# GT in five pieces of 512 columns and a turned strip, in place of ten pieces of 320

## The chip, the cores and the metric

The kernel runs on one core of a Trainium2 chip. A core has TensorE (PE in the profile, with PEld for its weight loads), VectorE (DVE), ScalarE (ACT), GpSimd (POOL) and SyncE (SP), each with an instruction queue of its own that runs in order, and DMA queues that SyncE and GpSimd feed. Times are device microseconds (us). The metric is the median time of the runs, and a profile of one execution goes with it.

## The reference

The output mixes two blocks over the same input x of 2,048 tokens by 640 columns; everything is float32.

```python
def _A_ref(x, wqkv, wo):            # 32 heads of 20 columns
    qkv = (x @ wqkv).reshape(B, S, 3, H, Dh).transpose(2, 0, 3, 1, 4)
    q, k, v = qkv[0], qkv[1], qkv[2]
    phi = lambda t: jnp.where(t > 0, t + 1, jnp.exp(t)) + 1e-6
    pq, pk = phi(q), phi(k)
    kv = jnp.einsum("bhsd,bhse->bhde", pk, v)
    z = jnp.einsum("bhsd->bhd", pk)
    num = jnp.einsum("bhqd,bhde->bhqe", pq, kv)
    den = jnp.einsum("bhqd,bhd->bhq", pq, z)[..., None] + 1e-6
    return (num / den).transpose(0, 2, 1, 3).reshape(B, S, D) @ wo
def _B_ref(x, w_gate, w_up, w_down):    # 1,536 hidden columns
    h = _sigmoid(x @ w_gate) * (x @ w_up)
    return h @ w_down
x = A_x
g = _sigmoid((x * gate_w).sum(-1, keepdims=True))
return g * _A_ref(x, A_wqkv, A_wo) + (1 - g) * _B_ref(x, B_w_gate, B_w_up, B_w_down)
```

## The kernel before

**Arithmetic.** A product is made of three matmuls (`mm3`, L407 to L409 in the profile): each operand is split into a high and a low part, and high by high, low by high and high by low are summed. A split takes ScalarE a copy to the high part (L420) and VectorE a subtraction for the low part (L424). So `woh`, `wol` are the two parts of rows of `wo`, `pkh`, `pkl` those of phi(k), `xnh`, `xnl` those of x.

**Phase 1.** No v is computed for the tokens. Since kv = pk^T (x Wv) = (pk^T x) Wv, the kernel accumulates GT = x^T pk, a 640 by 640 matrix, over the 16 tiles of 128 tokens, and multiplies it by Wv afterwards. `gt` lies in SBUF as 128 partitions by 5 blocks by 640 columns: rows are the columns of x, columns are those of k. The class `GTBatch` makes it in five batches: the tiles of block 0, of blocks 1 and 2, 3 and 4, 5 and 6, and (`glast`) of block 7, a block being two tiles. In each batch there is a result in PSUM for every unit u, one of five row blocks and one of two halves of 320 columns: ten units. `part` issues a unit's matmuls for some tiles, `out` adds the result to `gt` (a copy in the first batch). Between the units `order.fill()` lets other work in.

**The q steps.** Phase 1 is followed by `q_phase(1)`, a row of steps j = 0, 1, 2, ... that compute q for half of the tokens; its matmuls read splits of x's forms (`xah`, `xbh`, `xrh`, `xth`, `b12h`, ...) and of the weights' forms (`wg`, `wu`, `ws`, which are staged in `wst` and sent on to DRAM). Lists `extra[j]` put other work ahead of step j. `kv_part(hg)`, for six groups of heads that are 120 or 100 columns wide, multiplies `wv_sb` with the group's columns of `gt` (matmul L1578), masks the result with `bd` (`kvt`) and splits it (`kvh`, `kvl`). `m_part(hg)`, at j = 5, 6, 8, 10, 12 and 13, multiplies that with the group's rows of `wo`: six matmuls of 320 columns, whose results ScalarE copies to `ms` and GpSimd stores to `m_dram`.

**What sets the order.** The program's text doesn't fix all of it. A planner, the class `Order`, keeps estimated times for TensorE, ScalarE and VectorE as the program is built. Work that is not bound to a place is queued with its costs, perhaps with a key and a time from which it is ready; `fill` emits a queued item when its estimated end lies within a set slack of TensorE's. Items queued with `first=True` are looked at before others. `need(key)` emits an item at once if it has not been emitted yet. `queue_wo(hg)` queues the split of a group's rows of `wo` in this way, with the key ("wo", hg); `m_part(hg)` begins with `need(("wo", hg))` and ends with `queue_wo(hg + 2)`. All engines then run what was emitted, in that order. PSUM has eight result slots, rot0, rot1, dd0, dd1, ch0, ch1, cc0 and cc1; two of a name are used in turn (`ps_tile`).

Of the kernel before, what the change touches and what calls it, by code (L numbers as in the profile page):

```python
# [14 lines left out]
P = 128  # L15
# [4 lines left out]
TG = 512  # L20
# [347 lines left out]
def a_cost(w):  # L368
    return 0.06 + w / 1200

def v_cost(w):
    return 0.07 + w / 960

@with_exitstack
def gated_mix_kernel(ctx: ExitStack, tc: tile.TileContext, xt, xn, wk, wv, wo, wst_q, wst_f, out_t):
# [90 lines left out]
    z_dram = dram.tile([P // H, H, DH], F32, name="z_dram")  # L466
    m_dram = dram.tile([D, D], F32, name="m_dram")
    mr_dram = dram.tile([P, KC, D], F32, name="mr_dram")
    bdn = HPG * DH
# [504 lines left out]
    def queue_split(b):  # L974
        for s in range(2):
            order.add(a_cost(D), v_cost(D), lambda s=s: k_split(tok(b, s)), ("pk", b))

    class GTBatch:
        def __init__(self, n, blocks):
# [3 lines left out]
        def part(self, u, t0, t1, tag="rot", out=True):  # L983
            m, h = divmod(u, 2)
            cs = slice(h * HALF, (h + 1) * HALF)
            ms = slice(m * P, (m + 1) * P)
            if u not in self.ps:
                self.ps[u] = ps_tile(tag)
            ps = self.ps[u][:, :HALF]
            for n in range(t0, t1):  # L990
                i = self.tiles[n]
                mm3(ps, XN[i][0][:, ms], XN[i][1][:, ms], PK[i][0][:, cs], PK[i][1][:, cs],
                    n == 0, n == len(self.tiles) - 1)
            if t1 == len(self.tiles) and out:
                self.out(u)

        def out(self, u):
            m, h = divmod(u, 2)
            ps, dst = self.ps[u][:, :HALF], gt[:, m, h * HALF:(h + 1) * HALF]
            if self.n == 0 and u < 4:  # L1000
# [80 lines left out]
    order.slack(True)  # L1081
    for u in range(2 * KC):
        g.part(u, 0, 2, "rot" if u % 2 else "dd")
        order.fill()
# [3 lines left out]
    for c in range(1, 4):  # L1088
# [79 lines left out]
        else:  # L1168
            queue_xn(7)
        for u in range(6 if c == 1 else 4):  # L1170
            g.part(u, 0, 2, ("rot", "dd", "ch", "cc")[u % 4])
            if c == 1 and u == 0:
# [15 lines left out]
        for u in range(2 * KC):  # L1188
            g.part(u, 2 if u in g.ps else 0, len(g.tiles),
                   ("rot", "dd", "rot", "cc")[u % 4] if c == 3 or u < 8 else "rot")  # L1190
            order.fill()
            if u in (3, 5, 7, 9,):
                order.run("qw")
            if c == 2 and u == 9:
# [1812 lines left out]
```

## Time and profile before

| | before |
|---|---|
| median of 3 runs | 724.65 us (724.34 to 724.76) |
| span of the profiled execution | 722.5 us |
| median less span | 2.1 us |
| ScalarE, VectorE, TensorE busy in the span | 51%, 81%, 99% |
| DMA | 261 GB/s over the span |

The execution that was profiled is known by its span, from the first instruction to the last; its own time is not given apart. The stretch of the last batch of GT ends at 140.99 us of the span, and the first group of `m_part` begins at 157.66. Three more rows of the profile's groups show what the evacuations and the copies of `gt` are like: the operation, its operands, how often, its busy time in us and the mean of one in ns, then the idle time of the engine ahead of it and who ended that.

```profile
L424 DVE TENSOR_TENSOR tb<-rot,tb 128x512 f32<-128x512 f32 x56 | 36.1, 682 | 0.3 <-PE rot L409 0.3
L420 ACT ACTIVATE c<-ch 128x512 f32<-128x512 f32 x54 | 32.3, 597 | 84.2 <-PE ch L409 83.4
L424 DVE TENSOR_TENSOR hf<-c,hf 128x512 fp32r<-128x512 f32 x80 | 54.4, 687 | 19.3 <-ACT hf L420 18.9
```

### The profile page before, as it was taken

The page shows a single profiled execution, that of the slowest core. Times are in us where ns is not written, and L with a number is a line of the kernel's source. Part 1 is how long each engine was busy: PE and PEld are TensorE (multiplying, and loading weights), DVE is VectorE, ACT ScalarE, POOL GpSimd, SP SyncE. Part 2 cuts the span into 40 slices and gives each one's busy share as a digit, 9 for nine tenths or more (in the row PEclk, how much of TensorE's full clock was granted, in tenths as well). Part 3 has the DMA queues.
Part 4 walks back from the last instruction along what each step waited for, and adds up shares of the span by engine and source line. Part 5 has one row for each costly group of instructions (what it writes and reads, how often), then busy time and mean ns, then how long its engine had stood idle before and what let it go on. Part 6 is the DMA issues. An engine that isn't in the chain of part 4 may idle for free.

```text
span 722.5 us, 10190 instructions
## 1 busy us (share of the span) xinstructions
PE 718.2 (99%) x3539; PEld 616.7 (85%) x3539; DVE 587.1 (81%) x1028; ACT 370.0 (51%) x686; POOL 114.0 (16%) x184
## 2 busy tenths in 40 slices
PE   9999999999999999999999999999999999999998
PEld 8999999988888888888888888888888888888886
DVE  6898888988677989898989977447696968799895
ACT  6884748367556654545364664354423242454451
POOL 0211112113311212111210224001010101002200
PEclk9999999999999999999999999999999999999999
DMA  7677689598787866757687899968989895959947
GB/s 258 162 230 182 179 196 286 129 357 280 273 303 259 325 241 234 262 221 264 244 321 273 255 313 360 404 222 292 364 256 309 247 395 182 407 217 332 217 101 240
DMA packets 81690, 191.31 MB, mean 265 GB/s; under 512 B 12154, under 2 KB 40202, under 8 KB 77926
## 3 DMA queue, kind: packets, MB, share of 16 engines
q1 hardware_dynamic: 60726, 117.72, 49.6%
q0 software_dynamic: 20624, 72.70, 30.2%
q8 instruction: 28, 0.46, 0.3%
q10 hardware_dynamic: 288, 0.23, 0.1%
q14 instruction: 24, 0.20, 0.1%
HBM read 113.14 MB, written 75.20 MB: 261 GB/s over the span
## 4 chain that ended last, share of the span: by engine, by line
PE 99%; DMA 0%; DVE 0%; ACT 0%; issue 0%
PE ch L407 11%; PE ch L409 11%; PE ch L408 11%; PE cc L409 9%; PE cc L407 9%; PE cc L408 9%; PE dd L407 7%; PE dd L408 7%; PE dd L409 7%; PE rot L407 5%; PE rot L408 5%; PE rot L409 5%; PE rot L1578 1%; PE dd L2735 1%; PE ch L2735 0%; DMA xnh<-wk 0%
## 5 line engine op out<-in xcount | busy, mean ns | idle before, releaser
L420 ACT ACTIVATE c<-ch 128x512 f32<-128x512 f32 x54 | 32.3, 597 | 84.2 <-PE ch L409 83.4
L424 DVE TENSOR_TENSOR hf<-c,hf 128x512 fp32r<-128x512 f32 x80 | 54.4, 687 | 19.3 <-ACT hf L420 18.9
L420 ACT ACTIVATE hf<-c 128x512 fp32r<-128x512 f32 x80 | 48.9, 624 | 31.1 <-DVE c L424 31.0
L424 DVE TENSOR_TENSOR c<-cc,c 128x512 f32<-128x512 f32 x42 | 28.9, 688 | 28.3 <-PE cc L409 17.4
L407 PE MATMUL ch<-xth,ws 128*128 128x512 f32 x112 | 43.6, 389 | 0.0
L408 PE MATMUL ch<-xtl,ws 128*128 128x512 f32 x112 | 43.6, 389 | 0.0
L409 PE MATMUL ch<-xth,ws 128*128 128x512 f32 x112 | 43.6, 389 | 0.0
L424 DVE TENSOR_TENSOR c<-c,c 128x512 f32<-128x512 f32 x52 | 35.7, 687 | 3.3 <-ACT c L420 2.7
L424 DVE TENSOR_TENSOR tb<-rot,tb 128x512 f32<-128x512 f32 x56 | 36.1, 682 | 0.3 <-PE rot L409 0.3
L407 PE MATMUL dd<-xrh,wg 128*128 128x512 f32 x90 | 35.2, 391 | 0.0
L408 PE MATMUL dd<-xrl,wg 128*128 128x512 f32 x90 | 35.1, 390 | 0.0
L409 PE MATMUL dd<-xrh,wg 128*128 128x512 f32 x90 | 35.0, 389 | 0.0
L420 ACT ACTIVATE c<-dd 128x512 f32<-128x512 f32 x22 | 13.1, 596 | 41.4 <-PE dd L409 41.4
L407 PE MATMUL cc<-xbh,ws 128*128 128x512 f32 x84 | 32.7, 389 | 0.0
L408 PE MATMUL cc<-xbl,ws 128*128 128x512 f32 x84 | 32.7, 389 | 0.0
L409 PE MATMUL cc<-xbh,ws 128*128 128x512 f32 x84 | 32.7, 389 | 0.0
L424 DVE TENSOR_TENSOR tb<-dd,tb 128x512 f32<-128x512 f32 x36 | 24.7, 686 | 9.3 <-PE dd L409 9.2
L420 ACT ACTIVATE dd<-ch 128x512 f32<-128x512 f32 x22 | 12.8, 582 | 35.9 <-PE ch L409 35.9
L424 DVE TENSOR_TENSOR tb<-cc,tb 128x512 f32<-128x512 f32 x36 | 24.5, 684 | 1.9 <-PE cc L409 1.9
L424 DVE TENSOR_TENSOR wst<-wst 128x256 f32<-128x256 f32 (+1 forms) x65 | 24.6, 396 | 1.4
L409 PEld LDWEIGHTS ch<-xth,ws 128*128 128x128 f32 x112 | 21.0, 188 | 4.7 <-DVE ws L424 0.3
L408 PEld LDWEIGHTS ch<-xtl,ws 128*128 128x128 f32 x112 | 21.0, 188 | 4.3
(703 smaller groups left out, 2378.9 us busy)
## 6 DMA issues: line engine op xcount, KB each, us to landing
wf<-ws POOLq DMA_DIRECT2D x12, 1152.0 KB, 7.5
ws<-wf SPq DMA_DIRECT2D x11, 1152.0 KB, 8.8
wst<-wst_f SPq DMA_DIRECT2D x12, 640.0 KB, 4.9
wf<-wg POOLq DMA_DIRECT2D x12, 640.0 KB, 6.1
wd<-wd POOLq DMA_DIRECT2D x12, 640.0 KB, 8.1
wg<-wf SPq DMA_DIRECT2D x12, 640.0 KB, 6.9
wf<-wd SPq DMA_DIRECT2D x10, 640.0 KB, 11.0
xnst<-xn SPq DMA_DIRECT2D x16, 320.0 KB, 4.5
```

The lines of the kernel that those rows point to most:

```text
L407: nc.tensor.matmul(out, l_hi, r_hi, start=first, stop=False, skip_group_check=True)
L408: nc.tensor.matmul(out, l_hi, r_lo, start=False, stop=False, skip_group_check=True)
L409: nc.tensor.matmul(out, l_lo, r_hi, start=False, stop=last, skip_group_check=True)
L420: nc.scalar.activation(out, src, fn, **kw)
L424: nc.vector.tensor_tensor(out, a, b, op=op)
L1578: nc.tensor.matmul(ps[:w, :w], v[:, m, :w], gt[:, m, c0:c0 + w], start=(m == 0), stop=(m == KC - 1))
L2735: nc.tensor.matmul(ps, l, r, start=new, stop=j == 1 and k == ks[-1], skip_group_check=True)
```

## The change

The first 512 columns of GT are made in five units, one for each row block, 512 columns wide. The last 128 columns are made the other way round: pk's 128 columns are now the rows of the result and x's 640 columns run along it, in two units of 384 and 256 columns (`STRIP`). What arrives in `gt[:, m, 512:]` is thus a transposed block. After the last batch's two strip units, `gt_turn` turns it back: VectorE transposes within squares of 32 by 32, GpSimd writes the result to a new DRAM tensor `gt_dram` and reads it back in four pieces with the squares in their places, and ScalarE copies that to `gt`. The copy has the key "turn"; `extra[7]` needs it ahead of step 7. The heads' groups 4 and 5, which read columns from 512 on, move from steps 6 and 8 to 8 and 9, and group 3 stays.

```diff
+    gt_dram = dram.tile([P, D], F32, name="gt_dram")
...
+    STRIP = {KC: (0, 3), KC + 1: (3, KC)}
+    NU = KC + 2
+
+    def gt_turn():
+
+        turned = m1_tile("mb", "turned")
+        order.on_vec(D, "", 1.0, turned, gt[:, :, TG:])
+        nc.vector.transpose(turned.rearrange("p (b m c) -> p m b c", m=KC, c=H),
+                            gt[:, :, TG:].rearrange("p m (b c) -> p m b c", c=H))
+        gp.dma_start(gt_dram, turned)
+        back = m1_tile("mb", "back")
+        src = gt_dram.rearrange("(a r) (b n) -> b r a n", r=H, b=P // H)
+        for b in range(P // H):
+            gp.dma_start(back[b * H:(b + 1) * H].rearrange("r (a n) -> r a n", a=P // H), src[b])
+        order.add(a_cost(D), 0, lambda: act(gt[:, :, TG:].rearrange("p m (a c) -> p a m c", c=H),
+                                            back.rearrange("p (a m c) -> p a m c", m=KC, c=H), AF.Copy),
+                  "turn", lambda: order.when(back) + 1, first=True)
...
         def part(self, u, t0, t1, tag="rot", out=True):
-            m, h = divmod(u, 2)
-            cs = slice(h * HALF, (h + 1) * HALF)
-            ms = slice(m * P, (m + 1) * P)
             if u not in self.ps:
                 self.ps[u] = ps_tile(tag)
-            ps = self.ps[u][:, :HALF]
             for n in range(t0, t1):
-                i = self.tiles[n]
-                mm3(ps, XN[i][0][:, ms], XN[i][1][:, ms], PK[i][0][:, cs], PK[i][1][:, cs],
-                    n == 0, n == len(self.tiles) - 1)
+                x, pk = XN[self.tiles[n]], PK[self.tiles[n]]
+                if u < KC:
+                    ms = slice(u * P, (u + 1) * P)
+                    ps, l, r = self.ps[u], [t[:, ms] for t in x], [t[:, :TG] for t in pk]
+                else:
+                    b0, b1 = STRIP[u]
+                    ps = self.ps[u][:, :(b1 - b0) * P]
+                    l, r = [t[:, TG:D] for t in pk], [t[:, b0 * P:b1 * P] for t in x]
+                mm3(ps, *l, *r, n == 0, n == len(self.tiles) - 1)
...
-    tags = ["rot", "rot", "ch", "ch", "dd", "dd", "cc", "cc", "rot", "rot"]
-
-    for u in range(4):
+    tags = ["ch", "dd", "dd", "cc", "cc", "rot", "ch"]
+
+    for u in (KC, KC + 1, 0):
         glast.part(u, 0, 2, tags[u])
-    for u in range(4, 10):
+    order.add(0, v_cost(D), gt_turn, "turned", first=True)
+    for u in range(1, KC):
         glast.part(u, 0, 2, tags[u], out=False)
         order.fill()
-        if u == 5:
+        if u == 1:
             wg_split(("q", 1, KC - 1), w_stage)
-        elif u == 8:
-            glast.out(4)
-            glast.out(5)
-    p1_tail = [lambda u=u: glast.out(u) for u in range(6, 10)]
+        elif u == 3:
+            glast.out(1)
+    p1_tail = [lambda u=u: glast.out(u) for u in range(2, KC)] + [lambda: order.need("turned")]
...
-    for hg, (j, t) in enumerate(((1, "rot"), (1, "rot"), (3, "cc"), (6, "rot"), (6, "rot"), (8, "rot"))):
+    for hg, (j, t) in enumerate(((1, "rot"), (1, "rot"), (3, "cc"), (6, "rot"), (8, "rot"), (9, "rot"))):
         extra[j].append(lambda hg=hg, t=t: kv_part(hg, t))
+    extra[7].append(lambda: order.need("turn"))
```

The units of the batches between are issued in the same way, with other PSUM slots. The planner reckons with all of this, and so the order changes beyond the lines of the diff. Three places of it follow, one on each of three engines. A row names the line, the operation, its result and operands (with numbers of their tiles) and the shape of the result.

**TensorE, two units of one batch.** Before, in the last batch, the two tiles of one unit of 320 columns:

```order
L407 MATMUL rot0_1725<-pkh_1628,xnh_1600 128x320
L408 MATMUL rot0_1725<-pkl_1629,xnh_1600 128x320
L409 MATMUL rot0_1725<-pkh_1628,xnl_1601 128x320
L407 MATMUL rot0_1725<-pkh_1632,xnh_1625 128x320
L408 MATMUL rot0_1725<-pkl_1633,xnh_1625 128x320
L409 MATMUL rot0_1725<-pkh_1632,xnl_1626 128x320
```

After, in the last batch, from the second tile of the strip's unit of 256 columns (`ch1_1582`) to the whole of the first unit of 512:

```order
L407 MATMUL ch1_1582<-xnh_1503,pkh_1511 128x256
L408 MATMUL ch1_1582<-xnl_1504,pkh_1511 128x256
L409 MATMUL ch1_1582<-xnh_1503,pkl_1512 128x256
L407 MATMUL ch0_1590<-pkh_1507,xnh_1500 128x512
L408 MATMUL ch0_1590<-pkl_1508,xnh_1500 128x512
L409 MATMUL ch0_1590<-pkh_1507,xnl_1501 128x512
L407 MATMUL ch0_1590<-pkh_1511,xnh_1503 128x512
L408 MATMUL ch0_1590<-pkl_1512,xnh_1503 128x512
L409 MATMUL ch0_1590<-pkh_1511,xnl_1504 128x512
```

Where ten such units of six matmuls stood in the last batch, there are now seven. In the strip the moving operand is x and the one that is loaded is pk; over the whole kernel TensorE has 144 matmuls fewer.

**VectorE, in the q steps, around wol of group 0.** Before (`wol_1934` is group 0's, `wol_1966` group 1's):

```order
L424 TENSOR_TENSOR kvl_1911<-kvt_1908,kvh_1910 120x120
L424 TENSOR_TENSOR wol_1934<-wo_sb_1837,woh_1933 120x640
L424 TENSOR_TENSOR wst_1826<-wst_1826 128x256 x2
L424 TENSOR_TENSOR wst_1826<-wst_1826 128x128
L424 TENSOR_TENSOR xst_89<-xst_89 128x512
L428 SCALAR_TENSOR_TENSOR qe_1932<-qe_1932,qr_1944 128x512
L424 TENSOR_TENSOR wol_1966<-wo_sb_1841,woh_1965 120x640
```

After (`wol_1838` is group 0's; group 1's, `wol_1874`, follows two ws later; `qe_1778` is what was `qe_1964` before, made from the result rot0 of the same step):

```order
L428 SCALAR_TENSOR_TENSOR qe_1778<-qe_1778,qr_1792 128x512
L424 TENSOR_TENSOR kvt_1802<-cc1_1796,bd_65 100x100
L856 CAST kvh_1804<-kvt_1802 100x100
L424 TENSOR_TENSOR kvl_1805<-kvt_1802,kvh_1804 100x100
L424 TENSOR_TENSOR wst_1654<-wst_1654 128x256 x2
L424 TENSOR_TENSOR wst_1654<-wst_1654 128x128
L424 TENSOR_TENSOR xst_90<-xst_90 128x512
L424 TENSOR_TENSOR xz_1421<-xz_1421 128x512
L424 TENSOR_TENSOR xtl_1414<-xst_90,xth_1413 128x2x256
L424 TENSOR_TENSOR c11_1818<-dd0_1811,c11_1818 128x512
L424 TENSOR_TENSOR wol_1838<-wo_sb_1665,woh_1837 120x640
```

Group 0's wol has moved from ahead of the qe of the step's first result to behind c11, which reads the result (dd0) of the matmuls directly ahead of group 0's `m_part`.

**ScalarE, the same stretch and the next.** Before, from the stretch's start (woh of groups 0 and 1):

```order
L420 ACTIVATE wu_1885<-wst_1826 128x384
L420 ACTIVATE woh_1933<-wo_sb_1837 120x640
L420 ACTIVATE qe_1932<-dd1_1916 128x512
L420 ACTIVATE qr_1944<-dd1_1916 128x512
L420 ACTIVATE woh_1965<-wo_sb_1841 120x640
```

After, first the strip's copy and what is behind it, then woh of groups 0 and 1, then that of group 2:

```order
L420 ACTIVATE gt_86<-back_1629 128x4x5x32
L420 ACTIVATE qe_1754<-dd1_1738 128x512
L420 ACTIVATE qr_1758<-dd1_1738 128x512
L420 ACTIVATE wg_1779<-wst_1654 128x640
L420 ACTIVATE wu_1781<-wst_1654 128x384
```

```order
L420 ACTIVATE c11_1818<-ch0_1810 128x512
L420 ACTIVATE xth_1413<-xst_90 128x2x256
L420 ACTIVATE woh_1837<-wo_sb_1665 120x640
L420 ACTIVATE xth_1413<-xz_1421 128x2x256
L420 ACTIVATE ws_1849<-wst_1654 128x640
L420 ACTIVATE ws_1849<-wst_1654 128x512
L420 ACTIVATE ms_1843<-cc0_1844 120x320
L420 ACTIVATE ms_1843<-cc1_1860 120x320
L420 ACTIVATE woh_1873<-wo_sb_1669 120x640
```

```order
L420 ACTIVATE ms_1883<-dd1_1884 120x320
L420 ACTIVATE ms_1883<-dd0_1891 120x320
L420 ACTIVATE c22_1919<-ch1_1678 128x512
L420 ACTIVATE woh_1928<-wo_sb_1841 100x640
L420 ACTIVATE ms_1934<-dd1_1935 100x320
```

The woh of groups 0 and 1 have moved behind the results of the step ahead of their products, and that of group 2 stands behind c22, which reads the result (ch1) of the matmuls directly ahead of group 2's products. The copy of the strip stands ahead of the qe of dd1.

More of the change, by code (lines that the diff above doesn't have):

```diff
@@ L1081, in gated_mix_kernel @@
     order.slack(True)
-    for u in range(2 * KC):
+    for u in range(NU):
         g.part(u, 0, 2, "rot" if u % 2 else "dd")
@@ L1169, in gated_mix_kernel @@
             queue_xn(7)
-        for u in range(6 if c == 1 else 4):
-            g.part(u, 0, 2, ("rot", "dd", "ch", "cc")[u % 4])
+        first = 4 if c == 1 else 3
+        for u in range(first):
+            g.part(u, 0, 2, ("rot", "dd", "ch", "cc")[u])
             if c == 1 and u == 0:
@@ L1187, in gated_mix_kernel @@
             queue_forms(nx)
-        for u in range(2 * KC):
-            g.part(u, 2 if u in g.ps else 0, len(g.tiles),
-                   ("rot", "dd", "rot", "cc")[u % 4] if c == 3 or u < 8 else "rot")
+        for u in range(NU):
+            g.part(u, 2 if u in g.ps else 0, len(g.tiles), ("rot", "dd", "ch", "cc", "dd", "rot", "rot")[u])
             order.fill()
-            if u in (3, 5, 7, 9,):
+            if u > 2:
                 order.run("qw")
-            if c == 2 and u == 9:
+            if c == 2 and u == NU - 1:
                 queue_ls()
```

10 lines of the change are left out of this document (7 added, 3 removed).

## The prediction, made before the changed kernel was run

> **What bounds the kernel now.** I read the page first (span, busy shares, granted clock, the chain that ended last), then TensorE's waits, then the timeline around the end of GT and the first steps of q.
>
> ```profile
> span 722.5 us, 10190 instructions
> PE 718.2 (99%) x3539; PEld 616.7 (85%) x3539; DVE 587.1 (81%) x1028; ACT 370.0 (51%) x686; POOL 114.0 (16%) x184
> PEclk9999999999999999999999999999999999999999
> PE 99%; DMA 0%; DVE 0%; ACT 0%; issue 0%
> PE rot L496 <- PEq L2998: 0.8, 1, 0.8
> PE ch L1022 <- DVE k1h L855: 0.2, 1, 0.2
> ```
>
> TensorE is busy for 99% of the span at full granted clock. The last two lines are its whole list of waits (total, times, longest, in us): 0.8 and 0.2, both at the start. So the time is the sum of the matmuls' steps. Two things can change it: what the matmuls take, and a wait that TensorE does not have today. A faster VectorE or ScalarE brings nothing; a later one can cost at once. The profiled execution is given by its span alone, 722.5; the median of the timed runs, 724.65 (724.34 to 724.76), is 2.1 above it, which I take for what lies around the span in every run. The terms below are changes of the span; I add them to 722.5 and then the 2.1, which is the same as adding them to 724.65.
>
> **Term 1: the matmuls of GT.** Their price is the distance of starts, not the duration shown, since matmuls overlap.
>
> ```profile
> 130.40 0.31 PE L407 MATMUL dd<-pkh,xnh 128*128 128x320 f32 x1
> 140.85 0.30 PE L409 MATMUL rot<-pkh,xnl 128*128 128x320 f32 x1
> ...
> 146.76 0.40 PE L408 MATMUL dd<-xrl,wg 128*128 128x512 f32 x1
> 149.71 0.39 PE L409 MATMUL dd<-xah,wg 128*128 128x512 f32 x1
> ...
> 715.44 0.28 PE L407 MATMUL rot<-pq,ws 128*128 128x256 f32 x1
> 718.91 0.28 PE L409 MATMUL rot<-hf,wf 128*128 128x256 f32 x1
> ```
>
> Between the first two rows lie 71 steps of 320 columns: 10.45/71 = 0.1472 us. Between the next two, 13 of 512: 0.2269. Between the last, 29 of 256: 0.1197. For 384 no row exists; the line between 320 and 512 gives 0.1472 + 64 × 0.000415 = 0.1738. Per token tile of 128, before has 30 × 0.1472 = 4.416; after has 15 × 0.2269 + 3 × 0.1738 + 3 × 0.1197 = 4.284. That is 0.13 us for each of 16 tiles: **2.1 us less**. The columns streamed stay 9,600 per tile; what goes is the fixed part of 9 matmuls, about 14 ns each. If 384 falls on the line from 256 to 512 instead (0.1733), the gain is the same to a tenth; I take 1.8 to 2.2.
>
> The Trainium skill ("TensorE: Matmul & The Clock Gate", section "Wait — 56ns, not 53.3ns?") puts the fixed part of a warm matmul at about 2.5 ns; 144 matmuls fewer would then bring an estimated 0.4 us and not 2.1. The rows above disagree, and the rows decide, as these are this kernel's own operands.
>
> **Evacuations.** Ten results per batch become seven, on VectorE and ScalarE, which are not the bound. I walked GT's batches and the key/value products of head groups 0 to 2 with the pitches above: each result slot is free 0.3 us or more ahead of its next matmul. Cost 0; at the tightest place a late add would cost a few tenths.
>
> **Term 2: three new waits for wo's splits.** In the order of after, woh (ScalarE) and wol (VectorE) of head groups 0, 1 and 2 are issued directly ahead of the products that read them; before, groups 0 and 1 have theirs microseconds earlier.
>
> ```profile
> 146.53 0.74 ACT L420 ACTIVATE woh<-wo_sb 120x640 fp32r<-120x640 f32 x1 [0.76 <-DMA wo_sb<-wo]
> 149.97 0.82 DVE L424 TENSOR_TENSOR wol<-wo_sb,woh 120x640 fp32r<-120x640 f32 x1
> ...
> 153.11 0.39 PE L409 MATMUL rot<-b12h,wg 128*128 128x512 f32 x1
> 157.43 0.39 PE L409 MATMUL dd<-xrh,wg 128*128 128x512 f32 x1
> 157.81 0.31 PE L408 MATMUL cc<-wol,kvh 120*120 120x320 f32 x1
> 160.08 0.31 PE L408 MATMUL dd<-wol,kvh 120*120 120x320 f32 x1
> ```
>
> Before, wol of group 0 ends at 150.8 and is read at 157.81: 7 us of slack. After, it stands behind qe (which needs the last rot matmul, 153.11), kvt, kvh, kvl, three wst, xst, xz, one xtl and c. The prices of these, all from one stretch of before:
>
> ```profile
> 150.70 1.08 DVE L424 TENSOR_TENSOR wst<-wst 128x256 f32<-128x256 f32 x3
> 151.70 0.69 DVE L424 TENSOR_TENSOR xst<-xst 128x512 f32<-128x512 f32 x1
> 152.30 0.69 DVE L428 SCALAR_TENSOR_TENSOR qe<-qe,qr 128x512 f32<-128x512 f32 x1
> 155.64 0.26 DVE L424 TENSOR_TENSOR kvt<-cc,bd 100x100 f32<-100x100 f32 x1
> 156.35 0.69 DVE L428 SCALAR_TENSOR_TENSOR qe<-qe,qr 128x512 f32<-128x512 f32 x1
> 156.96 1.42 DVE L424 TENSOR_TENSOR ws<-wst,ws 128x640 fp32r<-128x640 f32 x2
> ...
> 150.19 0.60 ACT L420 ACTIVATE qe<-dd 128x512 f32<-128x512 f32 x1 [2.92 <-PE dd L409]
> 150.69 0.59 ACT L420 ACTIVATE qr<-dd 128x512 f32<-128x512 f32 x1
> 152.47 0.62 ACT L420 ACTIVATE xth<-xst 128x512 fp32r<-128x512 f32 x1
> 155.85 1.26 ACT L420 ACTIVATE ws<-wst 128x640 fp32r<-128x640 f32 x2
> 157.00 0.60 ACT L420 ACTIVATE c<-ch 128x512 f32<-128x512 f32 x1
> 158.30 0.88 ACT L420 ACTIVATE ms<-cc 120x320 f32<-120x320 f32 x2 [0.70 <-PE cc L409]
> 159.07 0.73 ACT L420 ACTIVATE woh<-wo_sb 100x640 fp32r<-100x640 f32 x1
> ```
>
> ScalarE reads a result 0.48 after its last matmul starts (149.71 to 150.19). In the clock of before: last rot matmul 153.11, ScalarE's qe 153.57, qr 0.50 later and 0.59 long, so VectorE's qe starts at 154.65. Then qe 0.61 (156.35 to 156.96), the kvt trio 0.71 (155.64 to 156.35), three wst 1.00 (150.70 to 151.70), xst 0.60 (to 152.30): 157.57. ScalarE's xth of that xst (0.62) holds xtl until about 158.33. Then xtl 0.60, c 0.60, wol 0.82: 160.35, and the matmul at 160.40 instead of 157.81: **2.6**. Least: only c's need of the dd matmul of 157.43 counts (0.45 + 0.60 + 0.82 + 0.05: 159.35), which is 1.5. Most: one wst or xst waits for its load as well, another 0.7: 3.3.
>
> Group 1 has its next wol on the heels of this one. Behind wol, VectorE does the second xtl (0.69); ScalarE's two ws write the memory that xtl reads, so they start at 160.96, take 1.15 (155.85 to 157.00), then ms, ms 0.77 (158.30 to 159.07), woh 0.73, and VectorE's wol 0.82: the matmul at 164.5. TensorE, shifted by 2.6, would be there at 160.08 + 2.59 = 162.7: **1.9** more. Least: ms waits only for the last product of group 0 (0.35 + 0.37 + 0.73 + 0.82 + 0.05 behind it), which leaves 0.7. Most: as reckoned.
>
> Group 2: its woh stands behind c, which needs the last ch matmul directly ahead of the products.
>
> ```profile
> 165.82 0.39 PE L409 MATMUL ch<-xth,ws 128*128 128x512 f32 x1
> 166.19 0.30 PE L408 MATMUL dd<-wol,kvh 100*100 100x320 f32 x1
> ...
> 166.25 0.60 ACT L420 ACTIVATE c<-ch 128x512 f32<-128x512 f32 x1 [3.06 <-PE ch L409]
> 166.74 0.73 ACT L420 ACTIVATE wg<-wst 128x640 fp32r<-128x640 f32 x1
> ```
>
> ScalarE's c starts at 166.25 and the next instruction at 166.74. In after that next one is woh, until 167.47; wol 0.82 and 0.05 on the way: the matmul at 168.35 instead of 166.19: **2.2**. This chain is short and has one value. Whoever waits behind these matmuls on TensorE is everything, as its queue runs in order. Sum of the three: 6.7, at least 4.4, at most 7.4.
>
> **Term 3: the strip's way through DRAM.** The transpose, one write, four reads and one ScalarE copy.
>
> ```profile
> L1542 DVE STREAM_TRANSPOSE zturn<-zperm x1: 835/835/835, 184.6 to 184.6; 128x640 f32<-128x640 f32 x1
> 138.00:142.00 4.00, 4.00 (x27) 3.83 (x26) 3.96 (x8) 2.71 (x5) 0.00 (x0) 1.00 0.10 17
> L364 POOL DMA_DIRECT2D p_dram<-qe x20: 539/544/572, 153.3 to 443.8; - x20
> DMA to landing us min/median/max: 2.3/5.9/12.5
> mr_dram<-m_dram POOLq DMA_DIRECT2D x4, 400.0 KB, 7.7
> ```
>
> The last batch is 60 matmuls ahead of 140.99, so it starts at 132.2. The strip comes first in it and takes 6 × 0.1738 + 6 × 0.1197 = 1.8. VectorE's two adds end at about 135.3, then come b12l, three xst and one 512 add at 0.60 each and wg at 0.73, and the transpose with 0.84: about 140. The DMA engines are nearly idle then (10%, 17 GB/s in the stretch shown). No row has transfers of 320 or 80 KB in such quiet; the nearest are those of the tile p_dram (the 2.3/5.9/12.5) and mr_dram's reads of 400 KB (7.7). For the write I take 3, near the shortest because of the quiet, with 2.3 and 5.9 as ends. Each of GpSimd's four issues takes 0.54, as for p_dram. The last read is taken at 5, the middle of 2.3 and 7.7, as SyncE's loads for q run by then: 150.2 in all. ScalarE's copy (about 0.7 for 640 columns, as woh) stands ahead of its qe of 150.19. A landing by 149.5 is free; until 150.8 ScalarE is late but TensorE not, since gt's copy, qe, qr, wg and VectorE's wg reach the matmul of 154.16 in time. Later than that, it costs one for one. I take **0**; from 0 up to 140 + 5.9 + 2.2 + 7.7 - 150.8 = 5.
>
> **Sum.** 724.65 - 2.1 + 6.7 + 0 = **729.3 us**; with the least waits 727.0, with the most 730.0.
>
> **Rivals.**
> *Nothing waits* (faster; chance 0.08). If wol of group 0 ended by 157.76 and those of groups 1 and 2 likewise, only term 1 stays: 722.6. For it: today's 7 us of slack and VectorE's 81%. Against it: the orders of the two kernels, in which c, a reader of the matmuls directly ahead, comes before wol on the same engine. It decides from the point where c's wait no longer holds wol.
> *Only group 2 waits* (0.09): the earlier two are covered by work that I have counted too long: 724.65 - 2.1 + 2.2 = 724.8. Against it: their lower bounds are above zero.
> *The forecast* (0.68): 727 to 731.
> *The strip comes back late* (0.13): slow DMAs, ScalarE's queue held, the matmul of 154.16 waits for wg: 2 to 5 more, 731 to 734.
> *The clock falls* (0.02). All tenths of PEclk are 9, and the longest wait today is 0.8, so no row shows what a wait of 2.6 does. If it halved the clock for as long as the three waits last, half of 6.7 would be lost again: 732.7. The Trainium skill (the same page, section "What's actually happening") states that the clock drops after an idle window of about 3.4 us; none of my three waits reaches that by itself, so by that rule nothing is lost here.
> *The change does less than it says* (within the forecast): if the price of a matmul were columns alone, 2.1 would go and 731.4 be left.
>
> **How the numbers follow.** About 0.2%, 1.45 us, is what a measurement of this kernel can tell from no change: faster is below 723.2, slower above 726.1. Faster holds the first rival, 0.09 with its edges; same holds the second, 0.09; slower the rest, 0.82. The range goes from 725.0 to 733.0: it holds the forecast with both ends of its waits and most of the late return, and leaves out the two fast rivals and the latest landings.
>
> **What would show it.** TensorE's list of waits should have three new rows: cc from VectorE's wol at about 2.6, and dd twice from wol or woh at about 1.9 and 2.2. The stretches of GT should be shorter by 2.1 in sum, with 512-column matmuls at 0.227 apart. ScalarE's copy gt<-back should be there between 149 and 151 less the gain, with or without a wait for the DMA. PEclk should stay at 9. If the list of waits holds nothing new, term 2 is wrong; if it names wg or qe behind back, term 3 is.

## The result, and the profile after

| | before | after |
|---|---|---|
| median of 6 runs | 724.50 us (724.19 to 724.94) | 738.14 us (734.14 to 741.18) |
| profiled execution | span 722.5 us | 739.13 us, span 737.4 us |
| ratio after to before | | 1.018, 95% interval 1.0162 to 1.0198 |

The change costs 13.6 us. The direction was forecast, the size was not: 729.3 was predicted, with 725.0 to 733.0 as the range. From the page of after, the busy times and the row of granted clocks:

```profile
PE 724.0 (98%) x3395; PEld 608.5 (83%) x3395; DVE 586.7 (80%) x1016; ACT 369.8 (50%) x685; POOL 117.0 (16%) x189
PEclk9999999989999999999999999999999999999999
```

TensorE has its 144 matmuls fewer and is still busy for 5.8 us longer (724.0 against 718.2). So two things grew: idle time, and the time that the remaining matmuls take. The row of clocks has a single 8 among its nines, which is easy to overlook. TensorE's list of waits in after (result, line, releaser; total, times, longest in us):

```profile
PE ch L407 <- ACT wg L420: 3.1, 1, 3.1
PE dd L407 <- ACT woh L420: 2.1, 2, 1.3
PE ch L407 <- ACT kb L420: 2.1, 1, 2.1
PE cc L408 <- DVE wol L424: 1.0, 1, 1.0
PE dd L408 <- DVE wol L424: 0.9, 2, 0.5
PE rot L497 <- PEq L3024: 0.8, 1, 0.8
```

The rows with woh and wol are the three waits of term 2. The one for wg (3.1) and the one for kb (2.1) are more. In TensorE's timeline of after (start, duration as shown, instruction, wait ahead of it) they stand here:

```profile
110.75 0.42 PE L407 MATMUL ch<-k2h,xth 128*128 128x322 f32 x1 [2.07 <-ACT kb L420]
...
158.74 0.79 PE L407 MATMUL ch<-xah,wg 128*128 128x512 f32 x1 [3.06 <-ACT wg L420]
...
166.62 0.41 PE L408 MATMUL cc<-wol,kvh 120*120 120x320 f32 x1 [1.03 <-DVE wol L424]
169.79 0.41 PE L407 MATMUL dd<-woh,kvh 120*120 120x320 f32 x1 [0.79 <-ACT woh L420]
170.65 0.41 PE L408 MATMUL dd<-wol,kvh 120*120 120x320 f32 x1 [0.45 <-DVE wol L424]
177.29 0.39 PE L407 MATMUL dd<-woh,kvh 100*100 100x320 f32 x1 [1.31 <-ACT woh L420]
178.15 0.59 PE L408 MATMUL dd<-wol,kvh 100*100 100x320 f32 x1 [0.47 <-DVE wol L424]
```

The first matmul behind the wait for wg shows 0.79 where 0.40 is usual. The windows view shows why (stretch and its length; busy time of PE, PEld, DVE, ACT and POOL, with counts; the granted clock; the DMA share; GB/s). The stretches are 3.41 us long and begin where the clock was seen to change:

```profile
106.44:109.85 3.41, 2.25 (x16) 1.99 (x14) 1.98 (x5) 0.20 (x1) 0.00 (x0) 1.00 0.79 258
109.85:113.27 3.42, 2.52 (x17) 2.52 (x18) 3.32 (x9) 3.42 (x10) 2.26 (x4) 1.00 1.03 332
154.23:157.64 3.41, 1.45 (x13) 1.18 (x11) 0.00 (x0) 1.29 (x3) 0.00 (x0) 1.00 1.13 255
157.64:161.05 3.41, 2.31 (x6) 1.66 (x7) 2.89 (x6) 2.43 (x5) 1.65 (x3) 0.50 0.46 139
161.05:164.47 3.42, 3.42 (x10) 2.65 (x9) 3.29 (x9) 1.19 (x3) 0.54 (x1) 0.50 0.98 377
...
174.71:178.12 3.41, 1.66 (x7) 0.89 (x5) 1.45 (x2) 1.22 (x2) 0.00 (x0) 1.00 0.86 300
178.12:181.53 3.41, 3.38 (x16) 3.38 (x17) 0.77 (x2) 2.49 (x5) 0.18 (x1) 0.50 0.28 86
```

The clock is at half for two stretches from 157.64, behind the wait for wg, and for one from 178.12, behind group 2's waits. TensorE is busy for 2.31 + 3.42 + 3.38 in these three, so about half of 9.1 is lost, 4.5 us as an estimate. With that, the whole time can be accounted for. The same matmul is looked up in both timelines, and the difference of its starts (after less before) is followed through the program:

| place (start before, start after) | difference, us | what was added since the row above |
|---|---|---|
| first matmul of GT (22.48, 22.24) | -0.2 | the start-up |
| ch<-k2h,xth (109.24, 110.75) | 1.5 | GT -0.5; the wait for kb 2.2 |
| first step of q (140.99, 142.31) | 1.3 | the last two batches of GT -0.2 |
| ch<-xah,wg of the wait (154.16, 158.74) | 4.6 | the wait for wg 3.3 |
| last but one of that step (157.21, 164.46) | 7.25 | half clock 2.7 |
| group 0, second matmul (157.81, 166.62) | 8.8 | wo's split 1.5 |
| group 1, second matmul (160.08, 170.65) | 10.6 | wo's split 1.8 |
| cc<-xth,ws (162.52, 172.30) | 9.8 | kv_part of group 4, done later now: -0.8 |
| group 2, second matmul (166.19, 178.15) | 12.0 | wo's split 2.2 |
| ch<-xtl,wu (168.07, 181.66) | 13.6 | half clock 1.6 |
| cc<-xbh,ws (169.92, 184.33) | 14.4 | kv_part of group 5, done a step later now: 0.8 |
| from 398.03 on (412.97) | 14.9 | small steps |

14.9 is the difference of the spans. Waits of the forecast's sum make 5.5 of it, waits that it put at nothing 5.5, the clock 4.3; GT gives back 0.7.

### The profile page after: what moved, and what is told of

Read it like the earlier page. It is cut to its first block, busy times and chain, and to the rows that moved or that the text cites. A ratio compares the mean times of both kernels' runs of the same rounds, so it can differ in the third digit from the quotient of the medians.

```text
span 737.4 us, 9903 instructions
## 1 busy us (share of the span) xinstructions
PE 724.0 (98%) x3395; PEld 608.5 (83%) x3395; DVE 586.7 (80%) x1016; ACT 369.8 (50%) x685; POOL 117.0 (16%) x189
## 4 chain that ended last, share of the span: by engine, by line
PE 94%; DMA 3%; DVE 2%; ACT 1%; issue 0%; SPq 0%; ACTq 0%; DVEq 0%
PE ch L407 11%; PE ch L408 11%; PE ch L409 11%; PE cc L407 9%; PE cc L409 8%; PE cc L408 8%; PE dd L408 7%; PE dd L409 7%; PE dd L407 7%; PE rot L407 5%; PE rot L409 5%; PE rot L408 5%; DMA wv_sb<-wv 1%; DMA qraw<-wst_f 1%; PE rot L1603 1%; DMA wq<-qp 1%
## 5 line engine op out<-in xcount | busy, mean ns | idle before, releaser
L407 PE MATMUL ch<-xah,wg 128*128 128x512 f32 x56 | 22.4, 401 | 3.1 <-ACT wg L420 3.1
```

What stands on the lines that cost most here:

```text
L407: nc.tensor.matmul(out, l_hi, r_hi, start=first, stop=False, skip_group_check=True)
```

## The experiments

**The theory** after the result: the way through DRAM costs most of the 14 us. Its reads land too late (the wait for wg); its DMAs make the planner reckon with later loads, so that it puts wo's splits directly ahead of their products; and the waits let the clock fall. The wait for kb is another matter: with seven units instead of ten, `order.run("qw")`, which issues q's loads between the units, comes later in a batch. **Rivals:** seven units with 512 columns bring the waits, whatever is done with the strip; or a single wait is the cause and the rest follows from it.

**1. The copy at need.** Only ScalarE's copy gt<-back is moved, to where step 7 needs it:

```diff
-                  "turn", lambda: order.when(back) + 1, first=True)
+                  "turn", lambda: 1e9, first=True)
```

> Strip's copy gt<-back issued by ScalarE only at step 7; the order of everything else is that of the changed kernel. Theory (each wait has its own cause): the wait of 3.1 us for wg at ch<-xah,wg and the half clock behind it (2.8 us) go; the wait at group 0's cc<-wol grows from 1.5 to at most 2.6, groups 1 and 2 stay at about 1.8 and 2.2. Time 5 below the changed kernel: about 733 us. Rival (the strip's landing is only the last of several late things in ScalarE's row): the wait at ch<-xah,wg stays near 3 with another releaser; 736 to 739 us.

Measured: 736.35 us (732.86 to 737.84), ratio 1.0147, 1.0116 to 1.0179. From TensorE's timeline of this run:

```profile
111.45 0.42 PE L407 MATMUL ch<-k2h,xth 128*128 128x322 f32 x1 [2.00 <-ACT kb L420]
...
162.57 0.41 PE L407 MATMUL cc<-woh,kvh 120*120 120x320 f32 x1 [1.19 <-ACT woh L420]
164.00 0.41 PE L408 MATMUL cc<-wol,kvh 120*120 120x320 f32 x1 [1.03 <-DVE wol L424]
```

The wait for wg is gone, and with it the half clock there. But group 0 now waits 1.19 and 1.03, and counting the spaced starts behind them it loses 2.6 (difference to before 3.56 ahead of the group, 6.19 in it); groups 1 and 2 lose 1.8 and 2.2. In after the late strip had hidden a part of group 0's wait. Here, behind much the same wait for kb as in after, the clock fell to half for 3.4 us, which cost 1.4, and it fell once more behind group 2. So 3.3 and 2.7 went, and only 1.8 of the median was won. By its waits the theory is right, but its 733 was missed, in part because it had no place for the clock behind kb.

**2. The splits early.** The three splits of wo and that of wg are forced ahead:

```diff
+    extra[1].insert(0, lambda: order.need(("wg", ("q", 1, 0))))
+    for hg, j in ((0, 1), (1, 3), (2, 5)):
+        extra[j].append(lambda hg=hg: order.need(("wo", hg)))
```

> Splits of wo for groups 0 to 2 (and wg ahead of them) forced early, strip's copy left where the change has it. Theory: the three waits at the products of groups 0 to 2 (1.5, 1.8, 2.2 us) and the second stretch at half clock (1.6) go; wg is split before ScalarE blocks, so its wait of 3.1 shrinks or goes as well. Time 729 to 733 us. Rival: woh of group 1 and what follows now stand behind the strip's late copy, so a wait of 1 to 3 us appears at the next product instead; 734 to 739 us.

Measured: 738.02 us (733.75 to 739.86), ratio 1.0175, 1.0137 to 1.0212. This missed the theory's 729 to 733. All waits for woh, wol and wg are gone, and others stand in their place: 3.5 at ch from ScalarE's xth and 3.6 at dd from VectorE's ms; the one for kb stays with 2.2. The clock fell to half behind all three. The first comes from the early split itself: in ScalarE's timeline group 2's woh waits 4.07 for its load until 166.74, and the xth that TensorE needs stands behind it. So a late split can't be mended by its place in ScalarE's queue alone, as long as its load isn't there. That is another cause than the rival's, which had the strip's late copy ahead of woh.

**3. q's loads earlier in a batch.**

```diff
-            if u > 2:
+            if u in (1, 2, 4, 6):
                 order.run("qw")
```

> The pieces of the q weights' split (qp) are issued after units 1, 2, 4 and 6 of a batch and not after 3, 4, 5 and 6; the q steps are as in the changed kernel. Theory: SyncE's load of qraw behind the stores of qp is issued 1 to 2 us earlier, and the wait of 2.1 us at ch<-k2h,xth goes; 736 us against about 738. Rival: the load itself is slow there and lands late whatever its issue; the wait stays at 1 to 2 us; 738 us.

Measured: 736.68 us (734.34 to 737.73), ratio 1.016, 1.0139 to 1.018. The wait for kb is gone: at the first step of q this run is 0.2 ahead of before, where after was 1.3 behind. That the place of `order.run("qw")` brings it is thus shown for this order. Of the median 1.5 was won, where 2 were expected. The profile is of the fastest of the four runs (734.34): in it the wait for wg is 1.2, and group 0 waits 2.3 for woh and 1.0 for wol, followed by half clock.

**4. Before, with late splits.** In the kernel before nothing is changed but the place of wo's splits for groups 0 to 2:

```diff
-            order.add(a_cost(D), v_cost(D), lambda: wo_split(hg), ("wo", hg), lambda: order.when(MO_AT[hg]), first=True)
+            order.add(a_cost(D), v_cost(D), lambda: wo_split(hg), ("wo", hg), lambda: 1e9 if hg < 3 else order.when(MO_AT[hg]), first=True)
```

> The kernel before, GT in pieces of 320, with the splits of wo for groups 0 to 2 issued only where their products need them. Theory: TensorE waits at the products of groups 0, 1 and 2, for about 1.5, 1 to 2 and 2.2 us, 4.5 to 6 in all, with no wait at ch<-xah,wg and none at ch<-k2h,xth; 729 to 731 us, plus up to 2 if the clock is halved after the third. Rival (the waits come from the strip and the changed order of VectorE, not from the place of the splits): under 1 us of waits, 724.5 to 725.5 us.

Measured: 735.14 us (734.75 to 735.34), ratio 1.0143, 1.0127 to 1.0158. The waits of this run:

```profile
PE dd L407 <- ACT woh L420: 3.8, 2, 2.5
PE cc L408 <- DVE wol L424: 1.4, 1, 1.4
PE dd L408 <- DVE wol L424: 0.9, 2, 0.5
```

They sum to 6.1, near the forecast's 6.7; by the ratio the kernel lost 10.4, more than the 731 to 733 expected. Most of the rest is clock: half from 166.1 to 169.5 and from 176.4 to 179.8, behind the waits of groups 1 and 2, where one such stretch had been reckoned with. With neither strip nor wide pieces, the late splits alone can cost most of what the change costs.

**5. Three edits together.** The edits of 1 and 3, and the planner's clocks moved so that the splits come early in its order:

```diff
+    order.pe += 11
+    order.act = order.pe - 1
+    order.vec += 13
```

> Three edits at once: strip's copy at step 7, qp after units 1, 2, 4 and 6, and the planner's estimated times of TensorE, ScalarE and VectorE set 11 to 13 us on ahead of the q steps, so that it emits the splits of wg and wo where their loads land. Theory (the pieces of 512 save 0.9 us, all the rest is waits and the half clock behind them): no wait of TensorE over 1 us, clock 1.000, 723.5 to 725.5 us. Rival (the strip or the new order of VectorE costs time in other places too): waits of 2 us or more remain, 727 us or more.

Measured: 729.23 us (726.02 to 730.02), ratio 1.0056, 1.004 to 1.0072. The granted clock is 1.000. The five waits of the change are gone; 1.7 at cc from kvt, 1.3 at ch from c and 0.8 at dd from c are new. The time is the rival's, though no wait comes to the rival's 2 us. ScalarE's woh of group 1 waited 3.22 for its load until 154.52, which the next run tests as the cause of the first.

**6. That split a little later.** As 5, with `order.when(MO_AT[hg]) + 4 * (hg == 1)` for group 1's split.

> As e6_all_three, but the split of wo for group 1 is due 4 us later, so that ScalarE's woh no longer stands ahead of qe and qr of rot while its load is on the way. Theory (the wait of 1.7 us at cc<-woh comes from that load, which lands 11 us after its issue among the strip's reads): this wait goes, those of 0.8 and 1.3 us at dd and ch are left or smaller; 725 to 727.5 us, clock 1.000. Rival (VectorE has too much to do there whatever ScalarE's order): a wait of 1.5 us or more stays at cc or dd; 728 to 730 us.

Measured: 728.56 us (727.55 to 730.26), ratio 1.0059, 1.0046 to 1.0073. The wait at cc for kvt is gone, as the theory said; 1.1 from c, 0.9 from ms and 0.5 from c stay later in the q steps, and by the ratio the time is that of 5. The strip's four reads still took 7.6 to 8.5 us to land in this run, and nothing on TensorE waited for them. This run shows GT's gain undisturbed. The same matmul, the first of the q steps, in the timeline of before and of this run:

```profile
140.99 0.39 PE L407 MATMUL ch<-xah,wg 128*128 128x512 f32 x1
```

```profile
140.13 0.39 PE L407 MATMUL ch<-xah,wg 128*128 128x512 f32 x1
```

0.86 earlier, of which 0.09 was there at GT's first matmul (22.48 before, 22.39 here): GT is 0.8 shorter, not 2.1.

**7. The trip cut the other way.** The pieces of 640 bytes are put on the write side, and the read is one of whole rows:

```diff
-        gp.dma_start(gt_dram, turned)
-        src = gt_dram.rearrange("(a r) (b n) -> b r a n", r=H, b=P // H)
-        for b in range(P // H):
-            gp.dma_start(back[b * H:(b + 1) * H].rearrange("r (a n) -> r a n", a=P // H), src[b])
+        dst = gt_dram.rearrange("(b r) (a n) -> a r b n", r=H, a=P // H)
+        for a in range(P // H):
+            gp.dma_start(dst[a], turned[a * H:(a + 1) * H].rearrange("r (b n) -> r b n", b=P // H))
+        gp.dma_start(back, gt_dram)
```

> The strip's squares change places on the way into DRAM (four writes in pieces of 640 bytes) and not on the way out (one read of whole rows). Theory (the way back is late because it shares the DMA engines with SyncE's loads): the one read still takes 7 us or more to land. Rival (the four reads in pieces of 640 bytes are slow by themselves): it lands within 4 us, and the wait for wg shrinks by 3 us. The time is not what is asked: 733 to 741 us.

Measured, in one run: 739.04 us. The read landed 6.5 us after its issue at 147.17. Neither 7 or more nor 4 or less, and the wait for wg shrank by 1.4, to 1.7, where the rival had 3: it is nearer to the theory that the crowd of SyncE's loads makes the reads slow. The four writes in pieces of 640 bytes, issued from 140.65 on, took 2.1 to 4.0 to land, while the DMA engines were at 0.17 of their time from 140 to 142 and at 0.73 in the 2 us after; the read of whole rows met 0.99 to 1.12. So small pieces alone don't make a transfer slow; whether they have a part in the crowd isn't decided.

**8 and 9. Why GT gains so little.** In one kernel the five units take pk's columns 128 to 639 and the strip takes 0 to 127, so that GT's columns stand in another order:

```diff
-                    ps, l, r = self.ps[u], [t[:, ms] for t in x], [t[:, :TG] for t in pk]
+                    ps, l, r = self.ps[u], [t[:, ms] for t in x], [t[:, P:D] for t in pk]
...
-                    l, r = [t[:, TG:D] for t in pk], [t[:, b0 * P:b1 * P] for t in x]
+                    l, r = [t[:, :P] for t in pk], [t[:, b0 * P:b1 * P] for t in x]
```

> The five units take pk's columns 128 to 639 and the strip columns 0 to 127 (GT comes out with its columns in other places, so the output is not the reference's); every instruction and its order is as in the changed kernel. Theory (512-column matmuls of GT are 0.232 apart because of where the moving operand begins): 0.227 apart, as in the q steps. Rival (it is the operands' tiles or the batch itself): 0.232 as before.

In the other x's 512 columns move and pk's 128 are loaded in these units:

```diff
-                    ps, l, r = self.ps[u], [t[:, ms] for t in x], [t[:, :TG] for t in pk]
+                    ps, l, r = self.ps[u], [t[:, ms] for t in pk], [t[:, :TG] for t in x]
```

> In the five units x's 512 columns move and pk's 128 are loaded (GT's five pieces come out turned, so the output is not the reference's); order and count are as in the changed kernel. Theory (the 0.232 belongs to pk as the moving operand): 0.227 apart. Rival (it belongs to the batches of GT whatever moves): 0.232. The time is 1 us below the changed kernel by the theory, equal by the rival.

Measured, one run each: 737.75 and 735.72 us; the distance of starts in the five units is 0.2310 to 0.2331 in the first and 0.2314 to 0.2345 in the second, batch by batch, as in after. Neither the columns nor which operand moves is the reason. The time of the second doesn't speak for the theory of 1 us less: one run lies within the 734.14 to 741.18 of the changed kernel, and its waits have other sizes (0.9 for kb, 1.2 for wg, 3.1 for group 0's woh). The cause is open.

**10. No trip.** The changed kernel with the DMAs through DRAM left out; ScalarE copies `turned`:

```diff
-        gp.dma_start(gt_dram, turned)
-        back = m1_tile("mb", "back")
-        src = gt_dram.rearrange("(a r) (b n) -> b r a n", r=H, b=P // H)
-        for b in range(P // H):
-            gp.dma_start(back[b * H:(b + 1) * H].rearrange("r (a n) -> r a n", a=P // H), src[b])
+        back = turned
```

> This leaves out the strip's way through DRAM alone (write, four reads and the tile `back`); ScalarE copies `turned` itself into GT's last 640 columns, so these columns aren't the reference's GT. All else is the changed kernel's, the planner included, which without these DMAs puts wo's splits ahead of their products again. Theory (the trip is what costs, both by its landing and by the splits that it pushes back): no wait at ch<-xah,wg and at the three wo products; what stays is the wait at ch<-k2h,xth (2.1 us) less GT's gain of 0.9: 725.5 to 727, and up to 728.5 if a stretch at half clock follows that wait as in e1_copy_late. Rival (the wo waits come from five pieces in place of ten, not from the trip): 2 us or more of waits remain at dd and cc from woh and wol, and the time is 730 or more.

Measured: 727.1 us (725.59 to 728.21), ratio 1.0035, 1.0022 to 1.0048; the profiled run is 725.59, its span 723.9. Its list of waits, whole, and then, from ScalarE's timeline, the copy and the splits of groups 0 and 1:

```profile
PE ch L407 <- ACT kb L420: 0.9, 1, 0.9
PE rot L497 <- PEq L3020: 0.8, 1, 0.8
```

```profile
140.66 0.74 ACT L420 ACTIVATE gt<-turned 128x640 f32<-128x640 f32 x1 [11.45 <-DVE turned L986]
147.30 0.74 ACT L420 ACTIVATE woh<-wo_sb 120x640 fp32r<-120x640 f32 x1 [1.21 <-DMA wo_sb<-wo]
151.86 0.74 ACT L420 ACTIVATE woh<-wo_sb 120x640 fp32r<-120x640 f32 x1
```

As the theory expected: the waits for wg and wo are gone without any edit to them, the splits of groups 0 and 1 are back at 147.30 and 151.86 (before: 146.53 and 151.83; after: 164.41 and 169.00), and the clock stays at 0.999. This profile is of the fastest of the four runs; another shows a clock of 0.997. **In the order of the changed kernel the way through DRAM costs 11.0 us of the medians (738.14 less 727.10).** The rival, that the units' shape brings the waits, falls for wg and wo. That the planner puts the splits back because of its own estimate of these DMAs' landings is read from its code; the run shows that they go back when the DMAs go in. It also takes out the DMAs and the planner's account of them together. Runs 5 and 6 bear on this: there the DMAs stay, the copy is at need and the planner's clocks are moved, and the waits for wg and wo are gone as well.

**11. No trip, and q's loads early.** As 10, with the edit of 3 and the copy at need.

> The same without the way through DRAM, with q's loads after units 1, 2, 4 and 6 as in e4_qw_early, and the copy issued at need. Theory: neither the wait for k2h nor those for wg and wo are left, and what is left of the change is GT's gain of 0.9 us by the traces: 723.3 to 724.5, ratio 0.998 to 1.000. By the forecast's own term 1 (2.1 us) it would be 722.4. Rival (other waits of the changed kernel remain that neither edit touches): 726 or more, with a wait of over 1 us in TensorE's list at some other place.

Measured: 727.49 us (725.08 to 730.16), ratio 1.0039, 1.0025 to 1.0052. The theory missed. In the profiled run, the slowest of eight, a wait for kb of 1.2 is still there although the load is issued at 101.21 (after: 101.75), since VectorE gets its data only at 108.50; and a new wait of 1.7 stands at ch behind ScalarE's c, which was held by a store of qe to p_dram until 189.68. So GT's gain did not come through in the time of this kernel either: here a load and a store are late, and the time varies by 5 us from run to run, against 1.1 for the kernel before, measured beside it. Run 6, the nearest that has the trip, is at 728.56, so in an order made for it the way through DRAM makes a difference of about 1 us and not 11 (ratios 1.0059 and 1.0039, with intervals that overlap). Most of the 11 is thus not the transfers' own time but what the order of the work puts behind them.

No version tried beats the kernel before.

## Why the prediction was wrong, step by step

| step of the prediction | forecast, us | measured in after |
|---|---|---|
| term 1, GT's matmuls | -2.1 (1.8 to 2.2) | -0.7 (0.8 undisturbed) |
| term 2, wo's splits | 6.7 (4.4 to 7.4) | 1.5 + 1.8 + 2.2 = 5.5 |
| term 3, the strip's return | 0 (to 5) | 3.3 |
| the walk through GT's batches | 0 | 2.2 (wait for kb) |
| the clock | 0 (rival: 3.4) | 2.7 + 1.6 = 4.3 |

Three terms that the prediction put at nothing make the miss: the strip's return, the walk through GT's batches and the clock, 9.8 us in all; term 1 was too large besides.

**Term 2 was right**, by mechanism and size. Group 2's 2.2 came out as worked; group 0's 2.6 did in the run without the late strip, and in after 1.1 less, since TensorE came late itself. Group 1 has 1.8, and the prediction's own terms give 1.8 too, where it wrote 1.9. Run 4 adds that such waits arise in the kernel before too, from the splits' place alone.

**Term 1 had the right mechanism and a wrong size.** It took the distance of 512-column matmuls from the q steps. In after's timeline, the start of the last batch's first unit of 512, the end of GT and a later q matmul:

```profile
135.32 0.39 PE L407 MATMUL ch<-pkh,xnh 128*128 128x512 f32 x1
142.31 0.39 PE L407 MATMUL ch<-xah,wg 128*128 128x512 f32 x1
145.48 0.40 PE L409 MATMUL dd<-xrh,wg 128*128 128x512 f32 x1
```

30 steps of GT take 6.99, so 0.2330 each; the next 14, in q, 3.17, so 0.2264. Over all batches GT's is about 0.232, and 384 and 256 columns have 0.175 and 0.119 (forecast 0.1738 and 0.1197). Per token tile that is 15 × 0.232 + 3 × 0.175 + 3 × 0.119 = 4.36 against 30 × 0.147 = 4.41: 0.05, or 0.8 for 16 tiles. The price had been taken from another place of the kernel than GT's batches, and it doesn't hold there.

**Term 3 failed in the landing.** The forecast had the write at 140, the reads' issue ended at 145.2, and 5 us for the last to land: 150.2. GpSimd's and ScalarE's timelines of after, and from the view of the tile back the landing of the four reads (shortest, median, longest):

```profile
141.52 0.60 POOL L364 DMA_DIRECT2D gt_dram<-turned  x1 [4.96 <-DVE turned L986]
144.88 2.23 POOL L364 DMA_DIRECT2D back<-gt_dram  x4 [2.76 <-ACT c L420]
...
156.35 0.74 ACT L420 ACTIVATE gt<-back 128x640 f32<-128x640 f32 x1 [8.22 <-DMA back<-gt_dram]
157.95 0.74 ACT L420 ACTIVATE wg<-wst 128x640 fp32r<-128x640 f32 x1
```

```profile
DMA to landing us min/median/max: 8.2/9.4/9.8
```

The write started 1.5 later and took 2.8, near the 3 of the forecast, but a read of 80 KB took 8.2 to 9.8 us. The windows of after for the write's start and for the reads, and for the second the shares of SyncE's queue (q1) and GpSimd's (q0), show the crowd:

```profile
140.00:142.00 2.00, 2.00 (x10) 1.64 (x9) 2.00 (x4) 0.00 (x0) 0.48 (x1) 1.00 0.00 0
144.00:156.35 12.35, 11.68 (x69) 9.98 (x67) 7.08 (x16) 3.70 (x7) 2.23 (x4) 1.00 1.05 266
q1 hardware_dynamic: 2381, 2.94, 93.3%
q0 software_dynamic: 192, 0.33, 11.3%
```

The DMA engines were idle when the write was issued and busy all the time that the reads took, 93% with SyncE's loads; no run takes these loads away. ScalarE's queue stood for 8.22 us with wg behind the copy, and TensorE got wg 3.06 late. The place of this wait and its chain were forecast (a rival with chance 0.13). The border from which it costs was 1 us later than the 150.8 that was said: from the copy's start to the matmul it is 2.39 (156.35 to 158.74), as the matmul waits for ScalarE's part of wg alone, so 151.8 for the matmul of 154.16. Wrong was to take the middle of 2.3 and 7.7 for a transfer in the fullest stretch, although the prediction itself says that SyncE's loads run by then. Run 10 shows that this price is not the only one: the same DMAs also bring term 2.

**The walk through GT's batches failed for q's loads.** It looked at result slots, and these were indeed never late. What it left out is what `order.run("qw")` issues between units: from the fourth of ten units on before, from the fourth of seven, which are wider, now. From SyncE's, VectorE's and ScalarE's timelines, first of before:

```profile
100.14 1.38 SPq L364 DMA_DIRECT2D qraw<-wst_f  x2
...
106.03 1.80 DVE L424 TENSOR_TENSOR qraw<-qraw 128x256 f32<-128x256 f32 x4 [2.32 <-DMA qraw<-wst_f]
```

and of after:

```profile
101.75 1.40 SPq L364 DMA_DIRECT2D qraw<-wst_f  x2
...
108.23 1.80 DVE L424 TENSOR_TENSOR qraw<-qraw 128x256 f32<-128x256 f32 x4 [1.33 <-DMA qraw<-wst_f]
...
109.65 0.72 ACT L420 ACTIVATE qp<-qraw 128x256 fp32r<-128x256 f32 x2 [4.06 <-DVE qraw L424]
110.28 0.75 ACT L420 ACTIVATE kb<-ch 128x322 f32<-128x322 f32 x2
```

The load is issued 1.6 later and lands 0.6 slower; VectorE's four adds and ScalarE's qp follow, kb stands behind qp in ScalarE's queue, and TensorE waits for kb until 110.75. ScalarE is busy for half of the span, and here its queue holds TensorE for 2 us, because the qp at its head waits, by way of VectorE's adds, for a load.

**The clock** was a rival with chance 0.02, on the ground that no single wait comes near 3.4 us. That reading was wrong: what counts is the idle time within a stretch of 3.41 us, of which half is enough (last section). That the size of the rival was near, 3.4 of loss there and 4.3 here, is luck: it was reckoned for other waits, and as half clock for as long as they last.

So the five errors add up: 1.4 less from GT, 1.2 less from wo, 3.3 from the strip, 2.2 from kb, 4.3 from the clock: 729.3 + 1.4 - 1.2 + 3.3 + 2.2 + 4.3 = 739.3, where the profiled execution has 739.13. The sum leaves out the start-up and the small steps of the table, which make 0.3, and what lies around the span, which is 1.7 in that execution (739.13 less 737.4) and not 2.1; these two nearly cancel.

## What to carry to other kernels

In a kernel whose TensorE is busy for 99%, a DMA that is added on the way to its operands has to be priced by a landing in the fullest stretch, by what stands behind its reader in an in-order queue, and where a planner knows of it, by what the planner then moves; leave out the DMA alone and see what else comes back. A wait of TensorE has a second price: where idle time came to half of a 3.4 us window of the clock here, up to 1.7 us more was lost, which a row of tenths hides. And a loop that issues loads by unit number changes their time when the units change.

## What the runs showed of the hardware

**The clock is granted by windows of 3.41 us that lie fixed in time, and in these traces half a window of idle time halved the next.** In each trace in which the clock changes on the way, the changes lie on one grid: in after 157.64, 164.47, 178.12 and 181.53, which are 2, 4 and 1 times 3.41 apart; in run 1 they are at 111.95 and, 19 windows later, at 176.80. Each run has its own grid. I cut TensorE's busy time along it between 60 and 230 us, in the twelve traces of after and the experiments. The windows at full clock in which TensorE was idle for 1.72 us or more, 14 in all, were each followed by one at half clock; the others, with 1.65 at most, by none. The two next to the bound, of run 7 and of the first kernel of 8 and 9, each with the window behind it:

```profile
153.85:157.26 3.41, 1.69 (x13) 1.09 (x11) 1.31 (x3) 3.41 (x7) 0.52 (x1) 1.00 0.56 134
157.26:160.67 3.41, 3.28 (x9) 2.60 (x9) 3.34 (x9) 1.36 (x3) 1.17 (x4) 0.50 0.79 308
```

```profile
108.40:111.81 3.41, 1.76 (x12) 1.50 (x11) 3.15 (x8) 1.94 (x7) 0.91 (x2) 1.00 0.99 303
111.81:115.22 3.41, 3.41 (x26) 3.41 (x25) 3.41 (x8) 3.38 (x8) 1.35 (x3) 1.00 0.99 354
```

Idle for 3.41 - 1.69 = 1.72, half clock; for 1.65, full clock. So the same waits can cost or not, by where a window ends: 2.07 for kb in after is cut by the border at 109.85 into 1.16 and 0.90, and nothing follows; 2.00 in run 1 lies in one window, and the next is at half clock. Group 2's pair of 1.31 and 0.47 was followed by half clock in after, run 1 and run 4, and was cut into 0.87 and 0.91 in run 3. From half clock it came back behind a window with at most 0.13 of idle time, and not behind one with 1.10 to 1.44. This would fit the spread of after's runs, 7 us against 0.75 before, as each run would meet the grid differently; that is not shown, and no run set the idle time alone, so the bound is read from these traces and not tested. The Trainium skill ("TensorE: Matmul & The Clock Gate", section "What's actually happening") has windows of 3413 ns that run freely, and the traces agree; it names an idle window as what brings half clock, and here half of one was enough.

**A read of 80 KB by GpSimd's queue took 8.2 to 9.8 us** with the DMA engines full, when its neighbour, a write of 320 KB that began with them idle, took 2.8 a few us earlier. The Trainium skill ("DMA: Bandwidth & Descriptors", section "Anatomy of one DMA — SWDGE (gpsimd) path") puts the fixed part of such a DMA at about 2 us; the write's 2.8, with its data, is in keeping with that, and the reads took several times as much.

**512-column matmuls have two distances**, about 0.232 in GT, whichever operand moves and whichever columns, and 0.2265 in most of q. The longer one isn't GT's alone: in before, the six of ch<-xth,ws between two groups of 320 columns, from 158.54 to 159.93, are 0.232 apart too. So q had rows at GT's price; why there are two is open.
